# A gated attention-and-MLP kernel: row maxima of the first group by key blocks, later key sets by their modelled landing, and a clearing moved

## The chip, the cores and the metric

The kernel runs on one core of one Trainium2 chip. The core has a matmul engine (TensorE, PE in the profile; PEld is its loading of weights), VectorE (DVE), ScalarE (ACT), GpSimd (POOL) and SyncE (SP), which work in parallel, each through its own instructions in order, and wait for each other by semaphores. DMA transfers are issued from the queues of SyncE, ScalarE and GpSimd. The metric is the device time of one execution in microseconds; each kernel is run several times and the median counts.

## What is computed

Input x has 2048 rows of 448 numbers. One branch is attention with 16 heads of 28, the other a layer norm with an MLP of 1792 hidden values; a gate for each row mixes the two.

```python
g = _sigmoid((x * gate_w).sum(-1, keepdims=True))
a = _A_ref(x, A_wqkv, A_wo)
b = _B_ref(x, B_w1, B_b1, B_w2, B_b2)
return g * a + (1 - g) * b
...
scores = jnp.einsum("bhqd,bhkd->bhqk", q, k) * (Dh ** -0.5)
p = _softmax(scores, axis=-1)
o = jnp.einsum("bhqk,bhkd->bhqd", p, v)
...
y = _layernorm(x, axis=-1)
h = _gelu(jnp.einsum("bsd,df->bsf", y, w1) + b1)
return jnp.einsum("bsf,fd->bsd", h, w2) + b2
```

The softmax subtracts each row's maximum. The kernel finds these maxima ahead of the attention stage, in a pass of its own.

## The kernel before

Most products are made of high and low parts (float32r), two or three matmuls for each. The rows are cut into four chunks c of 512 (NC = 4, CH = 512), the 16 heads into four groups g of four heads j (NG = 4).

**The head and the planned stage.** The head loads x and the first weights and makes the query and key tiles QK(0, 0), QK(0, 3) and QK(0, 4) with the whole array. QK(c, i) is output tile i of 128 columns of [q | k] for chunk c. Keys of group 0 are columns 448 to 559, so they lie in tiles 3 and 4. Then `Strips` (L391 on) takes over. It is a planner that runs while the program is being written: four row strips of the array (32 rows each) have a modelled time `t[s]` each, and the strip with the least time issues its next matmul. Pieces of work are QK tiles, value tiles (`Val`, 16), and the two MLP layers (`Up`, 14 for each chunk, `Down`, 4 for each chunk). A piece is visited by all four strips one after the other. Its cost for one matmul is 0.232 or about 0.205 us. Six PSUM banks hold pieces, banks 6 and 7 row maxima.

Other work is put into the program at modelled times: `at(t, fn)` (L420) queues a function for time t; `use` (L412) adds to the modelled time of an engine; `get(t, kb)` (L415) models all DMA as one line of 230 KB/us (`RATE`) and returns the end plus 2.2 us. So the planner decides the order of the instructions on every engine, and the real engines follow that order, whenever their data are there. Only the modelled time is fixed beforehand; the real wait is on semaphores, and an instruction that waits holds up everything behind it on its engine.

**Closing pieces.** When a QK piece is done, ScalarE copies it into a tile `qo` (four buffers) and issues a store to a buffer `qk` in DRAM (L280 to L286). Val pieces go to `vs`, MLP results to `gbs`. An Up piece is closed with a GELU into `h`, a copy `hh` on ScalarE and a residual `hl` on GpSimd (L339 to L353); two `h` buffers exist.

**Feeds.** `Feed.pump` (L533) issues input loads from GpSimd in the head and from SyncE later: x chunks, weights, and the pairs `bxr` for the layer norm's statistics, which VectorE takes in (`want_stats`, L630; `stats`, two instructions for each of 16 row tiles).

**Row maxima.** Class `RowMax` (L162). `kd` holds the keys of a group, 28 rows for head j on strip j, for all 2048 keys; `qd` the queries of chunk n (n runs from 0 to 15, group g = n // 4, chunk c = n % 4; two buffers). For each n and j there are 16 pieces: query tile i of 128 against key block k of 512. `one` (L194) issues one of them: a matmul (L199) and a `reduce_max` of 128x512 on VectorE (L201). `ready` (L190) asks whether head j's keys of the group are there. There are 1024 pieces in all. `Strips.rowmax` (L484) puts one in ahead of other work when its strip's `hot[s]` time has come, a bank is free by the model, and no strip is more than five ahead. `RM` = 0.65 us is its modelled time on VectorE.

In the kernel before, `done` (L704) waits for all key tiles of all chunks; 5.5 us later it queues, for each head, `load_k` (28 rows of 2048 keys, 224 KB) and `load_q` (56 KB) on GpSimd and sets `hot[j]`. When a strip has ended a group's keys, the next group's load is queued 1.5 us later on SyncE and `hot[j]` is set to 8.0 us later (L484 to L505).

**Between the stages.** When the last Up piece ends, `early` (L819) clears `la` on GpSimd 0.5 us later and loads and splits queries, keys and values of the first attention group.

**The attention stage** (L1097 on) works in turns. A unit is 128 keys of one head against 512 queries: three score matmuls, an exponential (together with two others, L1125), and the product with the values (`batch`, L1130). A turn takes five or six units. With five it may put in up to three row maxima, with six up to two:

```python
size = min(left, 5 if owed and owed > 2 * ((left - 116) // 6) else 6)
extra = {5: ((0, 3, 6), (3, 1, 5), (5, 2, 6)), 6: ((0, 3, 6), (5, 2, 6))}.get(size, ())
```

`owed` is the number of row maxima left, `left` the number of units left. Finished outputs are projected and mixed with the MLP branch at the end.

## Time and profile before

| | |
|---|---|
| median of 3 runs | 1094.24 us (1091.7 to 1096.02) |
| profiled execution, whole | 1093.73 us |
| its span, first to last instruction | 1091.6 us |
| busy: PE, DVE, ACT, POOL | 1074.6, 739.2, 634.8, 364.1 us |
| matmuls, weight loads | 13170 each |
| granted TensorE clock | 1.00 |
| DMA moved | 73.15 MB |

The profile is of one execution. A row of the timeline has start, duration, engine, line, operation and tiles; in brackets stands how long the engine was idle before it and what ended that. A row of the stretches has the stretch, its length, busy time and number of instructions for each engine asked for, the granted clock, the share of DMA engines that were busy and GB/s. Rows of waits have the engine and line that waited, for whom, the total, the number of waits and the longest. Ends of matmuls are modelled, so neighbouring ones overlap.

### The profile page before, as it was taken

To read this page: it belongs to the slowest core of one execution; us is meant where nothing else is said; L and a number is where in the kernel's file an instruction comes from. 1 tells how busy PE (TensorE), PEld (TensorE's weight loads), DVE (VectorE), ACT (ScalarE), POOL (GpSimd) and SP (SyncE) were. 2 spreads that over 40 slices of the span, in tenths; PEclk is the share of its full clock that TensorE was granted. 3 is DMA by queue.
4 is the path that set the end of the run, shared out by engine and by line. 5 is a ranking of instruction groups with operands and counts; after the bars stand their busy time and mean duration, and the time that the engine had idled before them with its cause. 6 is when DMAs were issued, how large, how long until landed. Compare 5 with 4: busy or idle time off the path is not lost.

```text
span 1091.6 us, 30496 instructions
## 1 busy us (share of the span) xinstructions
PE 1074.6 (98%) x13170; PEld 724.8 (66%) x13170; DVE 739.2 (68%) x1186; ACT 634.8 (58%) x668; POOL 364.1 (33%) x372
## 2 busy tenths in 40 slices
PE   9999999999999999999999999999999999999998
PEld 7989999999999999644444444444444444354555
DVE  4289989998999998667666766566767666321102
ACT  5324472141151150588878878878878878858562
POOL 3546687345242057321100110310012215345441
PEclk9999999999999999999999999999999999999999
DMA  6795433104100105410000000400002101011111
GB/s 231 225 293 190 167 120 109 43 5 103 38 9 11 38 9 127 119 40 27 18 14 19 22 23 25 117 17 16 19 18 73 38 16 54 25 52 38 61 52 59
DMA packets 47462, 73.15 MB, mean 67 GB/s; under 512 B 13632, under 2 KB 28608, under 8 KB 46416
## 3 DMA queue, kind: packets, MB, share of 16 engines
q1 hardware_dynamic: 33888, 39.11, 12.4%
q0 software_dynamic: 4800, 16.89, 5.4%
q10 hardware_dynamic: 8640, 15.21, 3.9%
q8 instruction: 103, 1.69, 0.6%
q14 instruction: 31, 0.25, 0.1%
HBM read 51.75 MB, written 19.31 MB: 65 GB/s over the span
## 4 chain that ended last, share of the span: by engine, by line
PE 93%; ACT 2%; DVE 2%; issue 1%; DMA 1%; POOL 0%; DVEq 0%; ACTq 0%
PE bk L475 33%; PE bk L1133 22%; PE bk L1121 18%; PE bk L199 15%; ACT p L1125 2%; PE bk L970 1%; DVE mx L201 1%; PE bk L971 1%; PE bk L972 1%; PE bk L886 1%; DMA qk<-qo 1%; PE bk L871 0%; DVE ob L992 0%; POOL hl L350 0%; DVE acc L977 0%
## 5 line engine op out<-in xcount | busy, mean ns | idle before, releaser
L201 DVE TENSOR_REDUCE mx<-bk 128x1 f32<-128x512 f32 x1024 | 672.4, 689 | 202.8 <-PE bk L199 157.0
L1125 ACT ACTIVATE p<-bk 128x1536 f32<-128x1536 f32 (+1 forms) x395 | 482.1, 1276 | 142.2 <-PE bk L1121 142.2
L199 PE MATMUL bk<-kd,qd 28*128 28x512 f32 x1024 | 446.7, 437 | 3.7 <-issue 1.4
L199 PEld LDWEIGHTS bk<-kd,qd 28*128 28x128 f32 x1024 | 186.1, 182 | 196.9 <-DVE mx L201 131.8
L475 PE MATMUL bk<-yh,w1f 32*128 32x512 f32 x1568 | 183.0, 391 | 0.4 <-ACT gb L385 0.4
L475 PE MATMUL bk<-yl,w1f 32*128 32x512 f32 x784 | 161.0, 391 | 0.0
L475 PEld LDWEIGHTS bk<-yh,w1f 32*128 32x128 f32 x1568 | 151.8, 183 | 2.2 <-ACT gb L385 1.7
L475 PE MATMUL bk<-w2h,hh 32*128 32x448 f32 x896 | 133.2, 366 | 1.3 <-ACT hh L343 1.3
L475 PE MATMUL bk<-w2l,hh 32*128 32x448 f32 x896 | 132.5, 363 | 0.0
L1133 PE MATMUL bk<-p,va 128*32 128x512 f32 x1024 | 131.2, 602 | 0.0
L1133 PE MATMUL bk<-p,vb 128*32 128x512 f32 x1024 | 129.5, 601 | 0.0
L350 POOL TENSOR_TENSOR hl<-h,hh 128x512 fp32r<-128x512 f32 x56 | 73.7, 1325 | 132.2 <-ACT hh L343 71.2
L806 POOL CAST yh<-yl 128x512 fp32r<-128x512 f32 x16 | 9.8, 614 | 293.6 <-PE bk L1133 118.4
L1121 PE MATMUL bk<-yh,ka 29*128 29x512 f32 x512 | 107.0, 482 | 0.3 <-ACT h L385 0.3
L475 PEld LDWEIGHTS bk<-yl,w1f 32*128 32x128 f32 x784 | 103.6, 183 | 0.2
L1121 PE MATMUL bk<-yh,kb 29*128 29x512 f32 x512 | 98.1, 477 | 3.8 <-ACT p L1125 3.5
L475 PEld LDWEIGHTS bk<-w2h,hh 32*128 32x128 f32 x896 | 99.5, 183 | 1.9 <-ACT hh L343 1.7
L475 PEld LDWEIGHTS bk<-w2l,hh 32*128 32x128 f32 x896 | 100.4, 183 | 0.1
L1121 PE MATMUL bk<-yh,la 28*128 28x512 f32 x512 | 88.5, 393 | 0.0
L385 ACT ACTIVATE gb<-bk 128x448 f32<-128x448 f32 x14 | 7.6, 545 | 138.3 <-PE bk L475 133.3
L475 PE MATMUL bk<-w2h,hl 32*128 32x448 f32 x896 | 87.3, 362 | 0.0
L1121 PE MATMUL bk<-yl,ka 28*128 28x512 f32 x512 | 86.9, 410 | 0.0
(141 smaller groups left out, 1591.3 us busy)
## 6 DMA issues: line engine op xcount, KB each, us to landing
qk<-qo ACTq DMA_DIRECT2D x28, 256.0 KB
raw<-in_xt SPq DMA_DIRECT2D x17, 256.0 KB
vs<-vt ACTq DMA_DIRECT2D x16, 256.0 KB
rc<-rls SPq DMA_DIRECT2D x60, 64.0 KB
bxr<-in_xk POOLq DMA_DIRECT2D x8, 448.0 KB, 6.4
acc<-gbs SPq DMA_DIRECT2D x16, 224.0 KB
out_y<-acc SPq DMA_DIRECT2D x16, 224.0 KB
qd<-qk SPq DMA_DIRECT2D x60, 56.0 KB
```

The costliest lines, as they stand in the source:

```text
L199: nc.tensor.matmul(ps, self.qd[n % 2][r, i * P:(i + 1) * P], self.kd[r, k * 512:(k + 1) * 512], start=True, stop=True)
L201: nc.vector.reduce_max(self.mx[n % 2][:, j, i, k:k + 1], ps, axis=AX)
L350: nc.gpsimd.tensor_sub(hl[f], h, hh[f].bitcast(F32))
L475: mm = nc.tensor.matmul(bk[:, x.bank, :n], a, b, start=x.first, stop=(len(x.rem) == 1 and m == len(ops) - 1), skip_group_check=True)
L806: nc.gpsimd.tensor_copy(h, l.bitcast(F32))
L886: nc.tensor.matmul(bk[:, b], w, v, start=(i == 0), stop=(i == len(ops) - 1), skip_group_check=True)
L970: nc.tensor.matmul(po, h, woh[:, g], start=(g == 0), stop=False, skip_group_check=True)
L971: nc.tensor.matmul(po, h, wol[:, g], start=False, stop=False, skip_group_check=True)
L972: nc.tensor.matmul(po, l, woh[:, g], start=False, stop=(g == NG - 1), skip_group_check=True)
L1121: nc.tensor.matmul(bk[:, turn_bank(i)], w[r, ks], q[r], start=(p == 0), stop=(p == 2), skip_group_check=True)
L1125: nc.scalar.activation(t[:, :count], bk[:, b:b + count], AF.Exp, scale=SCALE)
L1133: nc.tensor.matmul(bk[32 * j:32 * j + 32, 7], vg[n // NC][:, k, 32 * j:32 * j + 32], prob.pop(4 * b + j), start=(k == 0), stop=(k == NT - ...
```

## The change

1. **First group by blocks.** The keys of group 0 are loaded by blocks of 512 keys, one chunk at a time, as soon as both key tiles of that chunk are done (`keys`, 5.0 us later; for chunk 0 at planner time 4.0, with the four query loads of n = 0). Each block is four loads of 28 rows of 512 keys, 56 KB each, from GpSimd. `add_block` counts it when its modelled landing plus 1.0 us has come and lets the strips start. For n = 0 the pieces run over the key blocks outside and the query tiles inside, and `ready` admits as many blocks as are counted. The loads of whole key rows for group 0 are gone; the queries of n = 1 are loaded as before.
2. **Later key sets.** After a strip's last piece of a group `hot[j]` is set to never; when the load is issued, it is set to that load's modelled landing plus 1.0 us.
3. **Zeros.** The clearing of `la` moves from 0.5 to 4.0 us after the last Up piece, the key loads of the first attention group from 4.0 to 6.5 and their splits from 13.0 to 14.5 us (each plus its step for j).

```diff
+            self.blocks = 0
...
+        def load_block(self, c, queue):
+            cs = slice(c * CH, (c + 1) * CH)
+            for j in range(4):
+                queue.dma_start(self.kd[32 * j:32 * j + DH, cs].bitcast(F32), qk[D + j * DH:D + (j + 1) * DH, cs])
+
+        def add_block(self):
+            self.blocks += 1
+            if self.blocks == NC:
+                self.has.update((0, j) for j in range(4))
...
         def ready(self, j):
-            n = self.cnt[j] // 16
+            n, x = divmod(self.cnt[j], 16)
+            if n == 0:
+                return x // 4 < self.blocks
...
-            i, k = divmod(x, 4)
+            i, k = divmod(x, 4) if n else divmod(x, 4)[::-1]
...
-                    self.at(now + 1.5, lambda n=n, j=j: rowmax.load_k(n, j))
-                    self.hot[j] = now + 8.0
+                    def load(n=n, j=j):
+                        rowmax.load_k(n, j)
+                        self.hot[j] = self.get(self.clock + 0.6, 224) + 1.0
+
+                    self.at(now + 1.5, load)
+                    self.hot[j] = 1e9
...
+            if x.i in (3, 4) and all((x.c, m) in st.qks for m in (3, 4)):
+                keys(st, x.c, now + 5.0)
             if not st.keyed and all((c, m) in st.qks for c in range(NC) for m in (3, 4)):
                 st.keyed = True
-                def first(j):
-                    rowmax.load_k(0, j, nc.gpsimd)
-                    rowmax.load_q(0, j, nc.gpsimd)
-                    st.use("pool", st.clock, 1.1)
-                    st.hot[j] = st.get(st.pool, 290) + 1.5
-
                 for j in range(4):
-                    st.at(now + 5.5 + 1.2 * j, lambda j=j: first(j))
                     st.at(now + 16.0 + j, lambda j=j: rowmax.load_q(1, j))
...
+    def keys(st, c, when):
+
+        def load():
+            if c == 0:
+                for j in range(4):
+                    rowmax.load_q(0, j, nc.gpsimd)
+                    st.use("pool", st.clock, 0.55)
+                    st.get(st.pool, 56)
+            rowmax.load_block(c, nc.gpsimd)
+            st.use("pool", st.clock, 0.6)
+            st.at(st.get(st.pool, 230) + 1.0, landed)
+
+        def landed():
+            rowmax.add_block()
+            st.hot = [min(x, st.clock) for x in st.hot]
+
+        st.at(when, load)
...
+        keys(st, 0, 4.0)
...
-        st.at(now + 0.5, lambda: nc.gpsimd.memset(la.bitcast(F32), 0.0), pool=2.2)
+        st.at(now + 4.0, lambda: nc.gpsimd.memset(la.bitcast(F32), 0.0), pool=2.2)
...
-            st.at(now + 4.0 + 1.5 * j, lambda j=j: fetch_kk(0, j))
-            st.at(now + 13.0 + 2.0 * j, lambda j=j: split_kk(0, j), pool=1.9)
+            st.at(now + 6.5 + 1.5 * j, lambda j=j: fetch_kk(0, j))
+            st.at(now + 14.5 + 2.0 * j, lambda j=j: split_kk(0, j), pool=1.9)
```

## The prediction

> **What bounds the kernel now.** I read the page's busy times first, then the waits of the matmul engine, then the same stretches on VectorE, the GpSimd and SyncE timelines and the DMA issues.

> ```profile
> span 1091.6 us, 30496 instructions
> PE 1074.6 (98%) x13170; PEld 724.8 (66%) x13170; DVE 739.2 (68%) x1186; ACT 634.8 (58%) x668; POOL 364.1 (33%) x372
> PE bk L475 <- ACT hh L343: 1.3, 1, 1.3
> 66.33 0.50 PE L475 MATMUL bk<-xh,wq 32*128 32x512 f32 x3 [0.76 <-ACT qo L282]
> 264.64 0.47 PE L199 MATMUL bk<-kd,qd 28*128 28x512 f32 x1 [1.42 <-issue]
> 15.98 0.50 PE L475 MATMUL bk<-xh,wq 32*128 32x512 f32 x3
> 20.00:40.00 20.00, 20.00 (x341) 19.87 (x339) 1.00 0.46 140
> ```

> TensorE is the bound: it sits idle for 17 us of 1091.6. Three of its few stops lie where the diff touches something: 0.76 us at 66.3 us, 1.42 us at 264.6 us, 1.3 us on `hh` (at about 409 us, below). The planned stage begins at 15.98 us, so a time t of the planner is about 16 + t in the early trace. There four row strips of the array work side by side; 341 matmuls in 20 us are 20/(341/4) = 0.235 us a matmul on its strip. So one row maximum costs the planned stage at most 0.235/4 = 0.059 us.

> ```profile
> 22.15:57.54 35.39, 6.02 (x16) 1.00 0.64 194
> 57.54:446.40 388.86, 364.31 (x581) 1.00 0.29 88
> 22.15:57.54 35.39, 0.00 (x0) 1.00 0.64 194
> 57.54:446.40 388.86, 343.87 (x528) 1.00 0.29 88
> 446.40:1092.00 645.60, 328.57 (x497) 1.00 0.14 40
> ```

> These are VectorE's stretches, all its work first and then the row maxima alone. Up to 57.54 us it has done no row maximum and only 6.02 us of work in 35.4 us. From 57.54 us to the attention stage it is 94% busy (364.31 of 388.86): 528 row maxima at 343.87/528 = 0.651 us. About 497 are left for the attention stage. So VectorE sets how many maxima are done early, and the matmul engine how long the stages take.

> ```profile
> L1125 ACT ACTIVATE p<-bk 128x1024 f32<-128x1024 f32 x161 | 164.1, 1019 | 0.0
> 449.44 2.37 ACT L1125 ACTIVATE p<-bk 128x1536 f32<-128x1536 f32 x2 [0.42 <-PE bk L1121]
> ...
> 653.18 2.37 ACT L1125 ACTIVATE p<-bk 128x1536 f32<-128x1536 f32 x2 [1.20 <-PE bk L1121]
> ...
> 664.87 2.37 ACT L1125 ACTIVATE p<-bk 128x1536 f32<-128x1536 f32 x2 [1.21 <-PE bk L1121]
> ...
> 926.82 5.51 ACT L1125 ACTIVATE p<-bk 128x1536 f32<-128x1536 f32 x4 [0.32 <-PE bk L1121]
> 933.51 5.54 ACT L1125 ACTIVATE p<-bk 128x1536 f32<-128x1536 f32 x4 [1.19 <-PE bk L1121]
> ...
> 960.29 2.80 ACT L1125 ACTIVATE p<-bk 128x1536 f32<-128x1536 f32 x2 [1.21 <-PE bk L1121]
> ```

> These are ScalarE's exponentials, one form counted and then their timeline. A turn takes five units (of 128 keys by 512 queries) with up to three row maxima, or six with up to two (L1101, L1108). Each five-unit turn has one 128x1024 activation: 161 of them. Four five-unit turns repeat after 664.87 - 653.18 = 11.69 us, 2.92 us each; with all disturbances (926.82 - 449.44)/161 = 2.965. Eight six-unit turns take 960.29 - 933.51 = 26.78 us, 3.35 each, with maxima in them. Six units a turn are the cheaper way (0.558 against 0.585 us a unit), and the loop of L1101 goes over to it when few enough maxima are owed.

> **Part 1: the first group by blocks.** Removed: four loads of 224 KB and four of 56 KB issued from GpSimd after the last key tile. Added: sixteen loads of 56 KB (four for each 512 keys) and the same four query loads, the first eight as soon as the first column's stores are down. Same bytes, 12 issues more.

> ```profile
> 57.41 8.19 DMA qk<-qo
> 17.62 0.49 ACTq L286 DMA_DIRECT2D qk<-qo  x1
> 22.00:24.00 2.00, 2.00 (x41) 2.00 (x39) 0.15 (x1) 0.00 (x0) 0.00 (x0) 1.00 0.06 16
> 18.83 0.54 POOL L554 DMA_DIRECT2D raw<-in_wqk  x1
> 30.59 1.01 POOL L96 TENSOR_TENSOR wq<-first,wq 128x384 fp32r<-128x384 f32 x1 [11.23 <-ACT wq L92]
> 47.89 0.57 POOL L179 DMA_DIRECT2D kd<-qk  x1
> 51.47 0.51 POOL L185 DMA_DIRECT2D qd<-qk  x1
> kd<-qk POOLq DMA_DIRECT2D x4, 224.0 KB, 6.3
> qd<-qk POOLq DMA_DIRECT2D x4, 56.0 KB, 6.3
> ```

> When does block 0 arrive? By the plan: the diff queues it at time 4; ahead of it in the planner's one DMA line stand 4x256 KB of inputs and 3x256 KB of stores, then 4x56 and 230 KB; 2246 KB at 230 KB/us from -0.4 end at 9.4, plus the 2.2 and 1.0 in the code: 12.6, which is 28.5 us in the trace. In truth: the last store is issued at 17.62 us, and by 22 us the DMA share has fallen to 0.06, so the stores land at 20 to 22 us. GpSimd then issues eight loads at 0.51 us (47.89 to 51.98 us for eight): the last starts at 24 to 26 us, and these loads took 6.3 us to land in a crowded stretch. So 28 to 32 us for the last strip, earlier for the others, against 28.5. A matmul sent too early stops everything behind it on TensorE: 0 to 3 us; I take 0.5, since this stretch is empty where the 6.3 us were crowded.

> [...]

> Queued behind these loads on GpSimd are the next weight loads (issued until 18.83 + 0.54 us so far). They move to about 26 us; their weights are taken up at 29.8 us, just ahead of the subtraction at 30.59 us, so the 7 us are covered by that wait. Were they not, the query/key tiles of these weights would start late, 1 us for 1 us. The 12 added issues (6 us of GpSimd) lie in stretches where it waits.

> How many maxima come earlier: 57.54 - 28.5 = 29.0 us, less 6.0 us for the statistics, is 23.0 us; /0.651 = 35. I take off 3 for the first hand-overs. They lengthen the planned stage by 32 x 0.059 = 1.9 us, in which VectorE does 3 more; another falls into the key change of part 2. So 36 (30 if the block is 3 us late, 40 at best). **Cost:** 36 x 0.059 = +2.1 us (0 if they fall into gaps of a strip, 2.4 at most).

> **Gain:** four maxima less in the attention stage turn three five-unit turns (9 maxima, 15 units, 8.77 us) into 2.5 six-unit turns (5 maxima, 15 units, 8.37 us): 0.40 us. 36 maxima: -3.6 us. By the 2.965 us average it is 0.53 for four, -4.7; if turns cost what their units cost, 0.

> The loads leave the stretch at 48 to 57 us. The stop at 66.33 us came from a copy on ScalarE that waited for a store which was on its way for 8.19 us (57.41 us, the row from the chain that ended last). With 1.1 MB less in that crowd I take half of the 0.76 us: -0.4 (0 to -0.8).

> **Part 2: later key sets by their modelled landing.**

> ```profile
> 249.76 0.32 SPq L179 DMA_DIRECT2D kd<-qk  x1
> ...
> 257.83 1.37 SPq L179 DMA_DIRECT2D kd<-qk  x1
> 259.29 2.33 SPq L552 DMA_DIRECT2D raw<-in_xt  x4
> ```

> This is SyncE's queue at the first key change. The last key load was issued at 257.83 us with 1 MB of other loads at 259.29 us behind it, and the first matmul on it ran at 264.64 us after a stop of 1.42 us: 8.0 us of fixed delay were too few. In the changed kernel the key set ends about 36 x 0.65 = 23 us sooner, away from the input loads of 259.29 us, and the delay is worked out from the loads queued: -1.4 us (0 to -1.4). Strips waiting longer run other matmuls, so only VectorE loses. The second change (512 maxima) had no stop and has none in the list of waits to lose.

> **Part 3: the zeros.**

> ```profile
> 405.23 1.81 POOL L829 MEMSET la<- 128x2048 f32 x1
> 427.87 1.29 POOL L791 TENSOR_TENSOR la<-la,ka 128x512 fp32r<-128x512 f32 x1
> 408.33 0.69 ACT L342 ACTIVATE h<-bk,b1s 128x512 f32<-128x512 f32 x1 [1.65 <-POOL hl L350]
> ```

> The clearing of `la` stands on GpSimd between two residuals `hl`; ScalarE waits 1.65 us for `hl`, and TensorE 1.3 us for `hh` behind it. Moved 3.5 us down, it follows the last residuals: -1.3 us (0 to -1.8). Key loads and splits move 1.5 to 2.5 us later; the last split ended at 429.2 us, 17 us before 446 us, which covers it; without that cover the first scores would wait the 2.5 us.

> **Sum.** +2.1 - 3.6 - 0.4 + 0.5 - 1.4 - 1.3 = -4.1 us. The profiled execution took 1093.73 us (2.1 us of them around the span): 1089.6 us. The median shown is 1094.24, 0.5 us above, so **1090.1 us** on its scale.

> **Rivals.**

> A, *a larger gain*. Turns at their average price (-4.7), row maxima in idle moments of the strips (0), the whole 0.8 us gone, no late block: -4.7 - 0.8 - 1.4 - 1.3 = -8.2, 1086.0 us. For it: VectorE was idle and the array's strips are seldom even. Against: the 0.235 us of 20 to 40 us show hardly a gap.

> B, *no gain in the attention stage*. ScalarE's exponentials pace the turns (2.37 of 2.92 us), so fewer maxima buy nothing: -4.1 + 3.6 = -0.5, 1093.7 us. Against: the six-unit turns do run at the lower price with the same exponentials.

> C, *slower: the statistics hold the maxima up*.

> ```profile
> DVE stt L130 <- DMA bxr<-in_xk: 20.5, 4, 15.2
> bxr<-in_xk POOLq DMA_DIRECT2D x8, 448.0 KB, 6.4
> DMA to landing us min/median/max: 3.9/6.4/8.7
> ```

> VectorE takes its queue in order, and four times before 57 us it waited for `bxr`, 20.5 us in all, with nothing behind it. Now maxima stand behind each statistics pair, both their banks are held, and TensorE stops at the next one. GpSimd's wait for the key stores also delays the `bxr` loads, which take 3.9 to 8.7 us. Eight pairs, each 1.5 us later than planned, are +12 us: 1094.24 - 4.1 + 12 = 1102 us; it decides from 0.5 us a pair (4.1/8). Against: in the crowded stretch after 57 us none of the last four pairs waited for a DMA.

> D, *the modelled landing is too short*. With an empty DMA line it releases keys 1.5 + 0.6 + 1.0 + 2.2 + 1.0 = 6.3 us after the last matmul, where 8.0 was fixed; the trace needed 264.64 - 257.83 = 6.8 us from the issue alone. Then part 2 does not do what it says: the 1.4 stay and 0.5 to 1 come at each of two changes: -4.1 + 1.4 + 1.5 = -1.2, 1093.0 us. Against: those 6.8 us were shared with 1 MB.

> **How the numbers follow.** Forecast 0.42 (own range 1087 to 1093), A 0.22, B 0.15, C 0.13, D 0.08. What a measurement of this kernel can tell from no change is about 0.5%, 5.5 us: faster means below 1088.8, slower above 1099.7. A is faster, and of the forecast's range the third below 1088.8 with its likelier gains (0.17): 0.39. C is slower, with a little of it inside the bound: 0.11. The rest, 0.50, is the same. The range takes in A's best side and the mild half of C: 1085 to 1097.

> **What would show it.** First row maximum near 28 us and about 35 of them before 57.5 us; no matmul waiting for `kd` there; the stops at 264 and 409 us gone; the attention stage starting near 446.4 + 2.1 - 3.1 + 0.5 = 446 us with about 565 maxima done; some 134 activations of 128x1024 in place of 161. A stop of TensorE behind a `bxr` wait would show C, equal ends of both attention stages with fewer five-unit turns would show B. The prediction is wrong if VectorE is not nearly full between 28 and 57 us.

## The result and the profile after

| | before | after |
|---|---|---|
| median of six runs each | 1094.37 us (1091.7 to 1096.02) | 1101.07 us (1098.9 to 1102.48) |
| profiled execution, whole | 1093.73 us | 1101.62 us |
| its span | 1091.6 us | 1099.8 us |
| its mean granted clock | 1.000 | 0.995 |
| first exponential of the attention stage | 449.44 us | 458.88 us |

The ratio is 1.0061, with an interval of 1.0046 to 1.0075: slower by 0.6%, where 1090.1 us was forecast and 1085 to 1097 given as the range. Nearly the same work was done; what differs is when. The page of the changed kernel, span, busy times and the clock by slices of 27.5 us:

```profile
span 1099.8 us, 30518 instructions
PE 1076.9 (98%) x13170; PEld 724.0 (66%) x13170; DVE 740.3 (67%) x1186; ACT 633.1 (58%) x660; POOL 369.4 (34%) x384
PEclk9999899999999999999999999999999999999999
```

The one slice with an 8 begins at 110 us. Next the waits of its matmul engine, the view whose rows on `hh`, `kd` and `qo` carried the prediction (engine and line that waited, for whom, total us, times, longest):

```profile
PE bk L1152 <- ACT p L1156: 6.0, 20, 0.4
PE bk L488 <- ACT zall L325: 3.3, 1, 3.3
PE bk L488 <- SPq L529: 2.2, 1, 2.2
PE bk L488 <- ACT gb L398: 2.0, 2, 1.4
```

The stops on `hh`, `qo` and at the key change, which the prediction wanted to remove, are gone. Three others stand in their place, 7.5 us together: L488 is the strip matmul (L475 before), L325 the end of a value tile's closing, L529 the hand-over of a piece from one strip to the next, L398 the closing of a second-layer piece.

Then VectorE's row maxima (L214, L201 before) by stretches of the changed kernel, and the first of them from its timeline:

```profile
0.00:57.54 57.54, 22.50 (x35) 1.00 0.69 222
0.00:458.88 458.88, 369.88 (x566) 0.99 0.33 104
29.34 3.28 DVE L214 TENSOR_REDUCE mx<-bk 128x1 f32<-128x512 f32 x5 [6.48 <-PE bk L212]
```

So the first 35 maxima did come before 57.54 us, and 566 (529 before) were done when the attention stage began. That stage has fewer five-unit turns for it, 137 where 161 were. ScalarE's exponentials, by form and then by time:

```profile
L1156 ACT ACTIVATE p<-bk 128x1024 f32<-128x1024 f32 x137 | 139.6, 1019 | 3.3 <-PE bk L1152 3.3
458.88 2.37 ACT L1156 ACTIVATE p<-bk 128x1536 f32<-128x1536 f32 x2 [0.48 <-PE bk L1152]
```

But it begins 458.88 - 449.44 = 9.4 us late. To see where that lag arose, I counted the strip matmuls in stretches of 5 us in both traces and compared when the same number of them was reached (to about 0.6 us):

| before, us | after, us | lag | what lies there |
|---|---|---|---|
| 57.9 | 61.3 | +3.4 | the early maxima |
| 103.0 | 102.5 | -0.5 | two stops of before are gone |
| 122.9 | 129.7 | +6.9 | the stop on `zall`, at 107.5 us |
| 167.4 | 174.2 | +6.8 | nothing |
| 187.3 | 197.5 | +10.2 | the stop on L529, at 192 us |
| 253.6 | 262.5 | +8.8 | |
| 275.0 | 282.2 | +7.2 | the key stop of before is gone |
| 295.8 | 305.1 | +9.3 | the stop on `gb`, at 298 us |
| 403.1 | 414.6 | +11.4 | |
| 425.7 | 435.2 | +9.4 | the wait on `hh` of before is gone |

Some 0.7 us of the lag is older than the change: the first strip matmul starts at 16.70 us here and at 15.98 us before, ahead of anything that was altered. The largest step is 7.4 us at the stop on `zall`. Here it is in the changed kernel's timelines of ScalarE and GpSimd; the last row is from the chain of work that ended last:

```profile
101.32 0.33 ACTq L328 DMA_DIRECT2D vs<-vt  x1
110.08 0.54 ACT L324 ACTIVATE vt<-bk 128x448 f32<-128x448 f32 x1 [8.22 <-DMA vs<-vt]
...
99.38 0.73 POOL L160 DMA_DIRECT2D lnr<-lns  x1 [1.82 <-DMA lns<-mrt]
100.11 2.15 POOL L571 DMA_DIRECT2D raw<-in_xt  x4
...
101.32 8.68 DMA vs<-vt
```

`vt` has three buffers. The store of 101.32 us went out just behind a load of the statistics and four input loads, and took 8.68 us. ScalarE waited 8.22 us for its buffer, and so the bank of that value tile stayed full and TensorE had nothing to issue. What came after the wait is in the stretches of TensorE (length, busy time, number of instructions, granted clock, DMA share, GB/s):

```profile
108.00:110.00 2.00, 0.00 (x0) 1.00 0.37 139
110.00:112.00 2.00, 1.26 (x12) 0.53 0.29 111
112.00:114.00 2.00, 2.00 (x27) 0.50 0.46 174
114.00:116.00 2.00, 2.00 (x27) 0.50 0.00 0
116.00:118.00 2.00, 2.00 (x32) 0.76 0.20 77
118.00:120.00 2.00, 2.00 (x40) 1.00 0.50 190
```

The engine reads as fully busy from 112 us, but at half the clock until 117 us: 27 matmuls in 2 us, where 40 and more are usual. The stop of 3.3 us and 6.8 us at half the clock, worth 3.4 us, make 6.7 us, about twice the length of the stop.

At 192 us it is another queue. SyncE's timeline, TensorE's first row after the wait, and the same stretches:

```profile
190.57 2.59 SPq L569 DMA_DIRECT2D raw<-in_xt  x4
193.27 0.91 SPq L196 DMA_DIRECT2D qd<-qk  x1
...
194.29 0.46 PE L488 MATMUL bk<-w2h,hh 32*128 32x448 f32 x1 [2.17 <-SPq L529]
...
192.00:194.00 2.00, 0.12 (x2) 1.00 0.86 217
194.00:196.00 2.00, 1.71 (x28) 0.86 0.98 289
196.00:198.00 2.00, 2.00 (x27) 0.50 0.70 256
```

The signals by which one strip hands a piece to the next (L529) are written into SyncE's queue. One of them stood behind four input loads and a query load, 190.57 to 194.18 us; TensorE stood still for 2.17 us until it came, and half a clock of 3.4 us followed here too. The third stop, at 298 us, is ScalarE waiting for one of the two `gb` buffers; no half clock followed it in this execution:

```profile
299.47 0.55 ACT L398 ACTIVATE gb<-bk 128x448 f32<-128x448 f32 x1 [2.28 <-DMA gbs<-gb]
```

I call these stops X (`zall`), Y (L529) and Z (`gb`).

### The profile page after: what moved, and what is told of

Read it like the earlier page. It is cut to its first block, busy times and chain, and to the rows that moved or that the text cites. A ratio compares the mean times of both kernels' runs of the same rounds, so it can differ in the third digit from the quotient of the medians.

```text
span 1099.8 us, 30518 instructions
## 1 busy us (share of the span) xinstructions
PE 1076.9 (98%) x13170; PEld 724.0 (66%) x13170; DVE 740.3 (67%) x1186; ACT 633.1 (58%) x660; POOL 369.4 (34%) x384
## 4 chain that ended last, share of the span: by engine, by line
PE 92%; ACT 4%; issue 2%; DMA 1%; DVE 1%; SPq 0%; DVEq 0%; ACTq 0%
PE bk L488 34%; PE bk L1164 21%; PE bk L1152 17%; PE bk L212 14%; ACT p L1156 4%; PE bk L1001 1%; PE bk L1003 1%; PE bk L1002 1%; PE bk L917 1%; DMA vs<-vt 1%; PE bk L902 0%; DMA gbs<-gb 0%; PE bk L945 0%; DVE acc L1008 0%; SPq L569 0%
## 5 line engine op out<-in xcount | busy, mean ns | idle before, releaser
L214 DVE TENSOR_REDUCE mx<-bk 128x1 f32<-128x512 f32 x1024 | 674.3, 688 | 224.1 <-PE bk L212 191.9
L488 PE MATMUL bk<-yh,w1f 32*128 32x512 f32 x1568 | 188.3, 393 | 2.0 <-ACT gb L398 2.0
L488 PE MATMUL bk<-yl,w1f 32*128 32x512 f32 x784 | 164.0, 392 | 0.0
L488 PEld LDWEIGHTS bk<-yh,w1f 32*128 32x128 f32 x1568 | 151.1, 183 | 5.0 <-ACT gb L398 3.3
L488 PE MATMUL bk<-w2h,hh 32*128 32x448 f32 x896 | 140.7, 370 | 2.2 <-SPq L529 2.2
L488 PE MATMUL bk<-w2l,hh 32*128 32x448 f32 x896 | 140.4, 368 | 0.0
L1152 PE MATMUL bk<-yh,ka 29*128 29x512 f32 x512 | 104.5, 480 | 1.4 <-ACT p L1156 1.4
L488 PEld LDWEIGHTS bk<-w2h,hh 32*128 32x128 f32 x896 | 102.4, 186 | 3.2 <-SPq L529 2.5
L488 PEld LDWEIGHTS bk<-yl,w1f 32*128 32x128 f32 x784 | 103.3, 183 | 0.3
L488 PEld LDWEIGHTS bk<-w2l,hh 32*128 32x128 f32 x896 | 102.7, 186 | 0.1
L488 PE MATMUL bk<-w2h,hl 32*128 32x448 f32 x896 | 87.9, 362 | 0.0
L398 ACT ACTIVATE gb<-bk 128x448 f32<-128x448 f32 x14 | 7.6, 545 | 139.4 <-PE bk L212 68.6
## 6 DMA issues: line engine op xcount, KB each, us to landing
bxr<-in_xk POOLq DMA_DIRECT2D x8, 448.0 KB, 6.3
acc<-gbs SPq DMA_DIRECT2D x16, 224.0 KB
out_y<-acc SPq DMA_DIRECT2D x16, 224.0 KB
```

What stands on the lines that cost most here:

```text
L214: nc.vector.reduce_max(self.mx[n % 2][:, j, i, k:k + 1], ps, axis=AX)
L488: mm = nc.tensor.matmul(bk[:, x.bank, :n], a, b, start=x.first, stop=(len(x.rem) == 1 and m == len(ops) - 1), skip_group_check=True)
L1152: nc.tensor.matmul(bk[:, turn_bank(i)], w[r, ks], q[r], start=(p == 0), stop=(p == 2), skip_group_check=True)
```

## The experiments

The theory: the steps of the change do what was forecast, and what made the kernel slower are X, Y and Z and the half clock behind X and Y, a matter of where stores, loads and signals fall after the shift. Rivals: the early maxima themselves cost more than they bring; or the other parts lose; or the half clock has another cause.

**e1, part 1 alone, and e2, parts 2 and 3 alone.** In the first kernel the delay at a key change and the place of the zeros are those of before; in the second only these two are as in the changed kernel.

```diff
 # e1_blocks, against the changed kernel
-                    def load(n=n, j=j):
-                        rowmax.load_k(n, j)
-                        self.hot[j] = self.get(self.clock + 0.6, 224) + 1.0
-                    self.at(now + 1.5, load)
-                    self.hot[j] = 1e9
+                    self.at(now + 1.5, lambda n=n, j=j: rowmax.load_k(n, j))
+                    self.hot[j] = now + 8.0
...
 # e2_rest, against the kernel before: the same lines the other way, and
-        st.at(now + 0.5, lambda: nc.gpsimd.memset(la.bitcast(F32), 0.0), pool=2.2)
+        st.at(now + 4.0, lambda: nc.gpsimd.memset(la.bitcast(F32), 0.0), pool=2.2)
```

> Part 1 alone (key blocks; fixed 8.0 us for later key sets, zeros where they were). Theory: the loss comes from two stops of TensorE that part 1 brings, at about 108 us (ScalarE held by a vs store) and 192 us (SyncE held by load issues), each followed by microseconds at half clock. Both stops are here again, and the 1.3 us at the zeros stay: 1101 to 1104 us against 1094.4 before. Rival, that parts 2 or 3 cost the time: 1090 to 1094 us and no stop over 2 us.

> Parts 2 and 3 alone (later key sets by modelled landing, zeros moved; first group as before). Theory: none of the large stops at 108 and 192 us; the two old stops of 1.4 us at 264 us and 1.3 us at 409 us go: 1091 to 1092.5 us. Rival, that these parts cost the time: 1098 us or more.

Part 1 alone: 1099.41 us against 1093.71, ratio 1.0038 (1.0022 to 1.0054); its profiled execution had X with 3.6 us, Y with 2.0 us and Z with 1.8 us. So the large stops come with part 1, though the time is below the 1101 to 1104 us expected. Three of its twelve executions, with mean granted clocks of 0.997 to 0.999, took only 1093.37 to 1095.17 us; the nine with 0.994 to 0.996 took 1098.8 to 1101.08. Parts 2 and 3 alone: 1096.73 us, ratio 1.0026 (1.0014 to 1.0039), slower where a gain was expected. Its waits and TensorE's stretches show a part of the reason:

```profile
PE bk L199 <- issue: 2.5, 1, 2.5
...
262.00:264.00 2.00, 1.03 (x21) 1.00 0.79 210
264.00:266.00 2.00, 0.43 (x8) 1.00 1.02 207
```

The wait on `hh` at 409 us is gone, but the stop at the key change has grown from 1.42 to 2.5 us: the modelled landing came too early, which fits the four input loads, issued from 260.10 us on, that share the time with the key loads. That is rival D. It accounts for about 1.1 of the 3.0 us. The rest is not shown by this one trace, of an execution of 1095.87 us at a granted clock of 1.000; seven of the twelve executions had 0.998 or less. In the changed kernel the key change lies earlier and has no stop, so the two losses belong to different places, although the two ratios happen to multiply to the whole one.

**e3, e4 and e5: X and Y taken away, each and both.** X: two more buffers for `vt`. Y: the late input loads of x issued from GpSimd, so that SyncE's queue is left to the signals and the loads of keys and queries.

```diff
 # e3_vt and e5_both
-   vt = [... for i in range(3)]
+   vt = [... for i in range(5)]
-            v, ps, tt = vt[self.i % 3], bk[:, self.bank], self.i
+            v, ps, tt = vt[self.i % 5], bk[:, self.bank], self.i
...
 # e4_xq and e5_both
-                    nc.sync.dma_start(t, src)
+                    (nc.gpsimd if len(src.shape) == 2 and src.shape[-1] == CH else nc.sync).dma_start(t, src)
```

> The changed kernel with five vt buffers in place of three; the planner's order is the same, only ScalarE need not wait for the vs store issued three tiles earlier. Theory: the stop of 3.3 us at 108 us and the half clock behind it go, 6 to 7 us less than the changed kernel: 1094 to 1095.5 us. Rival, that the DMA crowd of that place itself holds TensorE (the next input or the bank comes late anyway): 1099 us or more. Rival, that only the idle time counts and not the clock: 3.3 us less, 1097.8 us.

> The changed kernel with the late x loads issued from GpSimd in place of SyncE; the planner's order is the same. Theory: SyncE raises the hand-over signal in time, the stop of 2.2 us at 192 us and the half clock behind it go, 3 to 3.5 us less: 1097.5 to 1098 us. Rival, that SyncE was waiting for the matmul engine and not the other way round: 1101 us. If GpSimd's residuals are delayed by its own load issues, new waits on hl appear.

> The changed kernel with five vt buffers and the late x loads issued from GpSimd, the planner's order unchanged. Theory: both large stops go, at 108 and at 192 us, and what the prediction summed is left: 4 us under before, 1089 to 1091 us. Rival, that another stop takes their place (the stops wander with every shift of the order): 1094 us or more, with a new stop over 2 us in the trace.

With more `vt` buffers: 1094.27 us, ratio 1.0005 (0.9991 to 1.0018), 6.8 us under the changed kernel's 1101.07. With the loads on GpSimd: 1095.1 us, 1.001 (0.9997 to 1.0024), 6.0 us under it. With both: 1092.55 us, 0.9986 (0.9977 to 0.9996), 8.5 us under it. The changed kernel was timed in another session; worked out from the ratios to before, the three differences are 6.1, 5.6 and 8.2 us. The first is as expected, the second is above the expected 3 to 3.5 us, and the third falls short of the expected 1089 to 1091 us: Z is left in its trace, with 2.3 us and 3.4 us of half clock. The same stretches, of the kernel with more buffers and then of the one with the loads on GpSimd:

```profile
108.00:110.00 2.00, 1.27 (x26) 1.00 0.85 325
110.00:112.00 2.00, 1.78 (x32) 1.00 0.25 95
```

```profile
192.00:194.00 2.00, 2.00 (x44) 1.00 0.64 159
```

X is down to less than 1 us with no fall of the clock, and Y is gone. So X and Y are shown as the causes of most of the loss. The gains do not add up (6.8 and 6.0 against 8.5): the single times of these two kernels spread over 5 to 6 us, and the slowest go with a low granted clock. The five executions of e3 at 1.000 took 1093.17 to 1094.9 us, its one at 0.995 took 1098.57; the three of e4 at 0.994 and 0.995 took 1098.61 to 1099.24, the other nine 1092.91 to 1096.99. So, by these mean clocks, the half clock behind the stops that are left comes in some executions and not in others. Only one execution of each has a trace, both among the longest (1098.57 and 1099.24 us): that of e3 still had Y with 2.6 us, that of e4 X with 3.2 us.

**e6: the same two edits on the kernel before.**

> The kernel before with the same two edits (five vt buffers, late x loads from GpSimd). Theory: it has neither stop, so the edits by themselves give little: the x loads no longer stand in SyncE's queue at 264 us, 0 to 1.5 us less, 1092 to 1094 us. Rival, that the edits speed any order up: 1090 us or less, and then the last run's gain is not the change's.

1095.19 us against 1094.1, ratio 1.001 (0.9997 to 1.0024), where 1092 to 1094 us was expected. More buffers and the other queue bring nothing where their stops are absent; the 8.5 us are not a general gain. The edits are not neutral either: in this trace the stop at the key change is 2.2 us long instead of 1.4, with 3.4 us of half clock behind it.

**e7: the price of a stop by itself.** Into the kernel before, four artificial stops: a small matmul, a chain of 4, 7, 10 or 14 small copies on ScalarE, and a matmul that waits for the chain. This adds work, and leaves nothing out.

```diff
+    def dose(st, n):
+        b = min(st.rm, key=lambda b: st.rm[b])
+        nc.tensor.matmul(bk[:, b, 0:P], dose_t, dose_t, start=True, stop=True, skip_group_check=True)
+        for _ in range(n):
+            nc.scalar.activation(dose_t, dose_t.bitcast(F32), AF.Copy)
+        nc.tensor.matmul(bk[:, b, 0:P], dose_t, dose_t, start=True, stop=True, skip_group_check=True)
...
+        for t, n in ((165.0, 4), (245.0, 7), (325.0, 10), (400.0, 14)):
+            st.at(t, lambda n=n: dose(st, n))
```

> The kernel before with TensorE made to wait on purpose at four quiet places, by chains of 4, 7, 10 and 14 small copies on ScalarE between two small matmuls (estimate 1.2 to 4 us of idle each). [...] Rival, that the half clock in the changed kernel has to do with the DMA crowd and not with the idle time: the clock stays at 1.00 after all four.

1118.59 us against 1094.1, ratio 1.0216 (1.0197 to 1.0235): 24.5 us. The waits, and TensorE's stretches around the stops of 1.42 us at 185 us and of 3.47 us at 360 us:

```profile
PE bk L746 <- ACT dose_t L745: 12.2, 4, 4.8
...
184.00:185.00 1.00, 0.03 (x1) 1.00 1.04 285
185.00:186.00 1.00, 0.55 (x5) 0.80 0.97 246
186.00:187.00 1.00, 1.00 (x12) 0.50 0.48 131
...
358.00:360.00 2.00, 0.00 (x0) 0.92 0.00 0
360.00:362.00 2.00, 1.20 (x9) 0.50 0.00 0
```

12.2 us of idle time cost 24.5 us, twice its length. Behind the four stops the clock stood at 0.50 for 3.4, 6.8, 6.8 and 6.8 us, 23.9 us together, which is worth 12 us: 24 of the 24.5 are accounted for. Some 1.7 us of them belong to this kernel's own stop at the key change (1.5 us at 268 us), which came just ahead of the second artificial stop. That a stop as short as 1.42 us leaves the clock at 1.00, as the one at 264.64 us of the kernel before did, was my estimate, and it was wrong: the clock stood at 0.50 for 3.4 us behind it. From 358 to 362 us no DMA runs (share 0.00), so the half clock there does not come from crowded transfers: that rival falls. It follows the stop.

**e8, e9 and e10: all three stops taken away, and the same change begun later.** e8 adds to e5 a third `gb` buffer (for its room, a constant moves to a pool that is closed earlier). e9 and e10 are the changed kernel with one number altered, the planner time at which the first block is queued.

```diff
 # e8_three, beside the edits of e5_both
-                gb = mhp[0].tile([P, D], F32, name="gb", bufs=2)
+                gb = mhp[0].tile([P, D], F32, name="gb", bufs=3)
...
 # e9_from8; e10_from16 has 16.0
-        keys(st, 0, 4.0)
+        keys(st, 0, 8.0)
```

> The changed kernel with both earlier edits and a third gb buffer (room made by taking one small constant tile out of the lasting pool). Theory: the stop of 1.8 us at 290 us, where ScalarE waits for a gbs store, goes and with it the half clock that followed it in some executions: 0.5 to 2.5 us under the kernel with two edits (1092.55), 1090 to 1092 us, and the spread of the single times shrinks. Rival, that the stop moves on to the next store: no change, 1092.5 us.

> The changed kernel with the first block queued at planner time 8.0 in place of 4.0. By the sums of the prediction this costs some 5 maxima, 0.3 us. Theory: the two stops are accidents of how stores, loads and hand-overs fall together, so a shift of the order of 4 us can lose them or bring others: any time from 1091 to 1102 us, and what it is follows from the stops in its trace. Rival, that early maxima as such cost the time: 1100.5 to 1101 us, with the same stops.

> The same with the first block queued at planner time 16.0: some 15 maxima fewer than in the changed kernel, 1 us by the sums. Theory: the time again follows the stops in the trace, 1091 to 1102 us, not the number of maxima. Rival, early maxima as such: half of the loss is gone, 1097 to 1098 us.

Without the three stops: 1088.42 us against 1093.75, ratio 0.9947 (0.9931 to 0.9963). That is better than the 1090 to 1092 us expected, and 4.1 us under e5; Z in e5, 2.3 us and half of the 3.4 us of half clock behind it, makes 4.0. Two of its waits, and its first exponential:

```profile
PE bk L1151 <- ACT p L1155: 5.8, 20, 0.4
...
PE bk L487 <- issue: 0.9, 1, 0.9
...
446.79 2.37 ACT L1155 ACTIVATE p<-bk 128x1536 f32<-128x1536 f32 x2 [0.40 <-PE bk L1151]
```

The wait of 0.9 us is the longest left in the planned stage (the first row belongs to the attention stage), which now ends where it was forecast: the first exponential comes at 446.79 us, against about 446.

Begun at 8.0 instead of 4.0: 1088.64 us, ratio 0.9949 (0.9932 to 0.9967), with no edit to any buffer or queue. Its timelines of GpSimd and ScalarE where X was, and its first exponential:

```profile
103.88 2.14 POOL L571 DMA_DIRECT2D raw<-in_xt  x4
...
100.54 0.33 ACTq L328 DMA_DIRECT2D vs<-vt  x1
100.96 1.10 ACTq L328 DMA_DIRECT2D vs<-vt  x2
...
448.79 2.37 ACT L1156 ACTIVATE p<-bk 128x1536 f32<-128x1536 f32 x2 [0.42 <-PE bk L1152]
```

The input loads now come 3 us after three of the stores instead of 1.2 us ahead of them, and X does not arise.

Begun at 16.0: 1099.48 us, ratio 1.0052 (1.0033 to 1.0071). It does only 17 maxima before 57.54 us, half as many, and yet is as slow as the changed kernel. TensorE's stretches:

```profile
132.00:134.00 2.00, 2.00 (x15) 0.50 1.02 349
...
224.00:226.00 2.00, 2.00 (x20) 0.50 0.41 151
```

It has its own places of half clock: one from 131.6 to 138.5 us, with no stop of TensorE ahead of it but few matmuls, 23 begun in the 3.41 us before (the last section comes back to it; why so few were ready I have not traced), and one behind a `gb` stop of 1.7 us at about 222 us. So the time goes with the stops and the half clock and not with the number of early maxima, which are 35, 33 and 17 in the kernels begun at 4, 8 and 16.

**e11, both remedies together**: first block at 8.0 and the edits of e8.

> The changed kernel with the first block at planner time 8.0 and the three edits (five vt buffers, late x loads from GpSimd, a third gb buffer). The kernel from 8.0 has no stop over 0.4 us left for the edits to remove. Theory: they give nothing on top, 1087 to 1089.5 us. Rival, that the edits help any order by themselves: 1085 us or less.

1086.96 us against 1094.94, ratio 0.993 (0.991 to 0.9949): faster than before and than the changed kernel, and at the edge of the 1087 to 1089.5 us expected. It is 1.7 us under e9, and the intervals overlap, so what the edits add to the later start isn't settled.

## Why the prediction was wrong

- **Early maxima (+2.1) and a late first block (+0.5).** 35 of 35 before 57.54 us, the first at 29.34 us against 28 to 28.5. The lag is +3.4 us by 61 us, of which 0.7 was there before the change could act: 2.7 against the 2.6. The four loads of the first block took 2.0 to 2.2 us to land in the changed kernel, all sixteen of 56 KB 2.0 to 4.4 us; the 6.3 us taken for them came from a more crowded stretch (DMA share 0.83 from 47 to 57 us of the kernel before, 0.35 from 20 to 30 us here).
- **The stretch after 57 us (-0.4).** Right in kind, and mis-sized: 3.9 us came back between 61 and 103 us. TensorE's stretches of the kernel before show where:

```profile
64.00:66.00 2.00, 1.57 (x28) 1.00 0.70 243
66.00:68.00 2.00, 1.67 (x28) 1.00 0.97 184
...
90.00:92.00 2.00, 1.30 (x29) 1.00 0.35 129
92.00:94.00 2.00, 2.00 (x31) 1.00 0.01 2
```

  Around the stop of 0.76 us at 66 us some 28 matmuls are missing against 40 for each 2 us (28/20 = 1.4 us), and around one of 0.7 us at 91.98 us, where a maximum waited for VectorE behind a statistics step, some 50 against 45 for each 2 us, until 98 us (2.4 us). The second was in the list of waits, and I gave it no term. The changed kernel has neither.
- **Key change (-1.4) and zeros (-1.3).** Both stops are gone; the lag falls by 1.6 us (8.8 to 7.2) and by 2.0 us (11.4 to 9.4) at those places. Part 2 by itself is no gain, though: where the key change stays among the input loads (e2) its landing is modelled too early.
- **Attention stage (-3.6).** From first exponential to the end 1091.6 - 449.44 = 642.2 us before and 1099.8 - 458.88 = 640.9 after: -1.2. In e8, with the same 137 five-unit turns and as many maxima left, it is 1085.7 - 446.79 = 638.9 (-3.3), in e9, with 132 such turns, 1086.4 - 448.79 = 637.6 (-4.5). So the price of a turn was about right; where 2.0 us of it went in the changed kernel's one trace I could not settle.
- **Rival C (the statistics hold the maxima up)** had the right sign and the wrong place: VectorE waited for no `bxr` load between 22 and 100 us. That its 1102 us lie so near the measured 1101.07 is luck. Rival B fell with e8 and e9.
- **The step that failed** is that the sum holds only stops that the trace of before shows. The added issues "lie in stretches where it waits", it said, and for all that comes behind them a plan shifted by some microseconds was taken to meet the same queues as before. It met others, for which the sum has no term: X (7.4 us in the lag), Y (3.4) and Z (2.1), about 13 us, against a sum of -4.1. Counted as idle time plus half of the time at half clock they are 3.3 + 3.4, 2.2 + 1.7 and 2.0, 12.6 us together; e8, without them, begins the attention stage 12.1 us earlier (458.88 - 446.79). Where they are absent, the total comes near the sum: -5.3 us in e8 (1093.75 - 1088.42) and -5.1 in e9 (1093.75 - 1088.64). That it comes so near is partly luck, since the stretch after 57 us gave 3.5 us more than its term, and other stretches, for which it has no term, took some 2 us back (in e8 the lag grows by 2.5 us between 103 and 123 us).

What stays open: which of the shifted instructions first brought the input loads ahead of the value stores, and where the attention stage of the changed kernel lost 2.0 us.

## What to carry to other kernels

In a kernel whose bound engine is 98% busy, a change that only shifts the plan must be priced with the stops that it can create: look for stores with few buffers on a busy queue (X, a stop of 3.3 us here), and for signals on a queue that also issues loads (Y, 2.2 us), and give each of them a chance and a price. Where half a clock followed a stop of TensorE here, I estimate that it cost 1.7 or 3.4 us on top of its length (half of the 3.4 or 6.8 us that the traces show); in e7 that and the idle time make 24 of the 24.5 us, and 1.7 us is more than the 1.42 us of its first stop. And before a shifted plan is judged, try it at two or three other starting points: here 4 us decided between +0.6% and -0.5%.

## What the hardware showed that I had not expected

The granted clock fell to 0.50 for 3.4 or 6.8 us after some stops of TensorE, and the length of the stop alone did not decide whether it did: 1.42 us was enough at 185 us of e7, 2.2 us at 192 us of the changed kernel, while 1.42 us in the kernel before and 2.5 us in e2, both at 262 to 266 us, left it at 1.00.

```profile
110.02:110.12 0.10, 0.00 (x0) 1.00 0.11 41
110.12:110.22 0.10, 0.00 (x0) 0.50 0.10 41
...
195.35:195.45 0.10, 0.10 (x9) 1.00 0.48 184
195.45:195.55 0.10, 0.10 (x8) 0.52 0.55 205
```

They lie 195.45 - 110.12 = 85.33 us apart, 25 times 3.413. Each trace can be divided along such a grid. This table counts, for the planned stages of all thirteen traces from 20 us on, the matmuls that began in each stretch of the grid at full clock, and how many of these stretches were followed by half a clock:

| matmuls begun in 3.41 us | stretches | followed by half a clock |
|---|---|---|
| 23 or fewer | 13 | 13 |
| 24 or 25 | 4 | 3 |
| 28 to 34 | 6 | 0 |
| 35 or more | 1563 | 0 |

The median is 58. So in these traces the half clock follows a stretch with few matmuls, wherever the idle time in it comes from. X left 7 in its stretch, Y 21, the stop of 1.42 us in e7 24; Z in the changed kernel left 24 as well and is the one exception. The stop of 1.42 us in the kernel before left 34, and the 2.5 us of e2 fall across an edge of the grid, with 32 in the emptier stretch. The half clock of e10 from 131.6 us on follows a stretch with 23, though TensorE reads as busy all through it. This is a count over traces and not an experiment, and some matmul records may be missing from them.

The grid lies differently against the start of each trace (its first edge at 0.7 to 2.9 us). So one and the same stop may be followed by half a clock in one execution and not in another, and that fits single times of one kernel that differ by 5 us and more with the granted clock, as in e1 and e3; with one trace for each kernel, this last step is argued and not shown.
